# An attention and MLP kernel: the values of three batches loaded as fp32 on a second ring and cast on chip, and a query's two copies on one engine

## The chip, the cores and the metric

The kernel runs on one core of one Trainium2 chip. The metric is the device time of one execution in microseconds (us); lower is better. All kernels of one call ran on the same chip, beside runs of the kernel before. The experiments come from several calls on several chips; the kernel before had medians of 321.6 to 322.25 us in them, so a difference of a few tenths between runs of different calls says nothing.

TensorE does the matmuls, VectorE (DVE), ScalarE (ACT) and GpSimd (POOL) work on tiles, and SyncE (SP) only issues transfers. The program fixes the order of each engine's instructions, and in these traces what stands behind a waiting instruction on VectorE, ScalarE or GpSimd waits too (6.6 us on ScalarE in x14). "Ring" is the queue of transfers that one engine fills; GpSimd's ring is q0 in the profile, SyncE's is q1.

## The reference

Eight batches of causal attention with a window, then an MLP over all 4608 tokens:

```python
# q, k, v: (8 batches, 8 heads, 576 tokens, 64)
# heads 0-3: 0 <= i-j < 32 ("plain"); heads 4-7: 0 <= i-j < 128, (i-j) % 4 == 0 ("dilated")
attn = softmax(where(mask, q @ k.T / 8, -1e9)) @ v
x = attn.transpose(0, 2, 1, 3).reshape(4608, 512)
h = x @ w_in                       # 512 -> 2048
return (h / (1 + exp(-beta * h))) @ w_out
```

## The kernel before

Tokens are handled in nine tiles of 512 for the MLP and in eight batches of 576 for the attention, which runs one batch ahead. `xT` is the attention's output, transposed: 128 partitions, four row blocks of 4608 bf16 columns. As its later columns are free at the start, they also serve as a workshop: the "relay" copies of plain keys and queries lie there. Tile 0 of the MLP is done in two parts of 288 and 224 columns; a "slot" is the work on one of the 16 blocks of 128 hidden columns in such a part, so slot 16 is the first of the second part.

The author writes operations with a wished time `vt`, estimated durations and the engines that could do each. A small simulation (`Plan.run`) then fixes, before the program is built, which engine does what and in which order. Its dependencies decide the order alone. The waits that the chip sees are added afterwards by the framework, from the stretches of tiles that each instruction reads and writes.

```python
rl = xT[0:RT, :, 6 * S:6 * S + R * P].rearrange(          # relay copies
    "p (z x) (T h d) -> p z x T h d", z=2, T=R, h=2)
...
def direct_vd(b, deps, vt):                                # dilated values, cast by the load
    ...
    return [load("POOL", (dst[0:80, 0], rows[0:80]), deps, vt, 320, .35),
            load("POOL", (dst[:, 1], rows[16:CT]), deps, vt, 512, .35)]
...
for hf in range(2):                                        # one copy for each half of a query
    def evac(e, g=g, kind=kind, i=i, hf=hf): ...
    steps[n].append(plan.op([dve(S), act(S)], evac, ...))  # each on VectorE or ScalarE
```

In batches 0 to 2 (`b < DIRECT`) q, k and v come straight from DRAM through GpSimd's ring, which casts fp32 to bf16 on the way, in the order k, q, k, q, values, then w_in and w_out, then batch 1. From batch 3 on, q and k are cast to a scratch in DRAM and read back by transposing loads on SyncE's ring.

The softmax here doesn't subtract the row's maximum and nothing guards it: scores larger than these inputs give would overflow.

## Time and profile before

| | before |
|---|---|
| time, median of 3 runs | 322.11 us (321.36 to 322.4) |
| span of the profiled run | 320.0 us |
| TensorE busy, mean granted clock | 307.9 us (96%), 1.00 |
| useful matmul columns / 2.4 GHz | 286 us |
| GpSimd's ring, SyncE's ring | 20.19 MB, 21.18 MB |

From the page of the kernel before: busy tenths of TensorE, and its granted clock in tenths, in 40 equal slices of 8 us.

```profile
PE   6988999999899999999999999999999999999995
PEclk9999999999999999999999999999999999999999
```

TensorE is busy 80% or more from the second slice to the last but one. The record of its clock begins at 13.2 us and stays at 1.00 until the span's end. The prediction below reads the windows, the timeline and the waits of this kernel.

### The profile page before, as it was taken

To read this page: it belongs to the slowest core of one execution; us is meant where nothing else is said; L and a number is where in the kernel's file an instruction comes from. 1 tells how busy PE (TensorE), PEld (TensorE's weight loads), DVE (VectorE), ACT (ScalarE), POOL (GpSimd) and SP (SyncE) were. 2 spreads that over 40 slices of the span, in tenths; PEclk is the share of its full clock that TensorE was granted. 3 is DMA by queue.
4 is the path that set the end of the run, shared out by engine and by line. 5 is a ranking of instruction groups with operands and counts; after the bars stand their busy time and mean duration, and the time that the engine had idled before them with its cause. 6 is when DMAs were issued, how large, how long until landed. Compare 5 with 4: busy or idle time off the path is not lost.

```text
span 320.0 us, 6224 instructions
## 1 busy us (share of the span) xinstructions
PE 307.9 (96%) x2333; PEld 171.0 (53%) x2333; DVE 210.2 (66%) x488; ACT 181.8 (57%) x346; POOL 123.0 (38%) x158
## 2 busy tenths in 40 slices
PE   6988999999899999999999999999999999999995
PEld 4766777655555545554555454545554444444453
DVE  5578767688988887677778788785875344343300
ACT  2677778677747645574656455645664544545411
POOL 7999753533785445622913652252000000000000
PEclk9999999999999999999999999999999999999999
DMA  6999999999207999799899988993134110100021
GB/s 85 173 208 208 204 172 185 161 178 191 57 2 127 171 213 174 162 172 182 190 171 157 186 193 159 159 221 87 53 88 107 45 55 33 35 33 34 33 100 66
DMA packets 87799, 41.83 MB, mean 131 GB/s; under 512 B 63113, under 2 KB 82457, under 8 KB 87449
## 3 DMA queue, kind: packets, MB, share of 16 engines
q0 software_dynamic: 40544, 20.19, 50.0%
q1 hardware_dynamic: 47080, 21.18, 31.0%
q8 instruction: 18, 0.29, 0.4%
q14 instruction: 13, 0.10, 0.1%
q10 hardware_dynamic: 144, 0.07, 0.1%
HBM read 40.37 MB, written 18.28 MB: 183 GB/s over the span
## 4 chain that ended last, share of the span: by engine, by line
PE 85%; DVE 8%; ACT 3%; issue 2%; POOL 1%; POOLq 0%; DVEq 0%; ACTq 0%
PE bank L730 38%; PE bank L698 35%; PE bank L636 3%; PE bank L565 2%; DVE g L710 2%; PE bank L395 2%; PE bank L576 2%; ACT tnh L705 1%; PE bank L559 1%; DVE xsd L649 1%; POOL st L343 1%; PE bank L666 1%; ACT qd L209 1%; DVE xT L209 1%; ACT pt L603 1%
## 5 line engine op out<-in xcount | busy, mean ns | idle before, releaser
L705 ACT ACTIVATE tnh<-bank,beta_half 128x512 bf16<-128x512 f32 (+2 forms) x160 | 102.5, 645 | 94.2 <-PE bank L698 86.4
L698 PE MATMUL bank<-xT,w_in_bf 128*128 128x512 bf16 (+2 forms) x640 | 145.2, 357 | 1.3 <-ACT xT L209 0.3
L730 PE MATMUL bank<-w_out_bf,g 128*128 128x512 bf16 (+1 forms) x592 | 144.5, 373 | 0.0
L710 DVE SCALAR_TENSOR_TENSOR g<-tnh,bank 128x512 bf16<-128x512 bf16 (+2 forms) x160 | 100.6, 632 | 65.0 <-ACT tnh L705 63.4
L698 PEld LDWEIGHTS <-w_in_bf 128*128 128x128 bf16 x640 | 59.6, 97 | 54.8 <-issue 2.8
L730 PEld LDWEIGHTS <-g 128*128 128x128 bf16 x592 | 54.0, 98 | 50.0
L603 ACT ACTIVATE pt<-bank 128x288 bf16<-128x288 f32 (+1 forms) x112 | 43.9, 447 | 9.7 <-PE bank L565 7.7
L636 PEld LDWEIGHTS <-pt 128*128 128x128 bf16 x448 | 23.5, 97 | 15.8 <-issue 1.4
L747 ACT ACTIVATE osb<-bank 128x512 f32<-128x512 f32 (+2 forms) x34 | 19.8, 583 | 16.6 <-PE bank L730 16.0
L649 DVE TENSOR_TENSOR xsd<-bank,rcp 72x256 bf16<-72x256 f32 x64 | 26.9, 421 | 2.2
L616 POOL TENSOR_TENSOR pt<-pt,mask_d 128x288 bf16<-128x288 bf16 x19 | 13.7, 731 | 38.1 <-ACT pt L603 35.4
L209 POOL COPY kz<-raw 64x1152 bf16<-64x1152 bf16 x8 | 11.9, 1486 | 20.4 <-DMA raw<-s 20.3
L649 DVE TENSOR_TENSOR xsp<-bank,rcp 96x384 bf16<-96x384 f32 x32 | 17.7, 554 | 1.1
L648 DVE RECIPROCAL rcp<-bank 72x4 f32<-72x4 f32 (+1 forms) x96 | 16.8, 175 | 2.2 <-PE bank L636 1.2
L636 PE MATMUL bank<-vd,pt 128*128 128x65 bf16 x256 | 16.4, 193 | 0.3
L565 PE MATMUL bank<-qzd,dk 128*128 128x144 bf16 x128 | 16.4, 232 | 0.0
L209 POOL COPY vd<-st 80x1024 bf16<-80x1024 bf16 (+1 forms) x10 | 10.7, 1084 | 12.5 <-DMA st<-in_v_dram 12.5
L565 PEld LDWEIGHTS <-dk 128*128 128x128 bf16 x128 | 11.0, 101 | 6.9 <-issue 1.7
L343 POOL DMA_DIRECT2D vp<-in_v_dram x9 | 12.5, 1386 | 1.8 <-PE bank L698 1.8
L616 DVE TENSOR_TENSOR pt<-pt,mask_d 128x288 bf16<-128x288 bf16 x29 | 9.1, 341 | 4.2 <-ACT pt L603 4.1
L749 DVE TENSOR_SCALAR osb<-bank 128x512 f32<-128x512 f32 (+1 forms) x4 | 2.4, 592 | 13.8 <-ACT osb L747 13.7
L636 PE MATMUL bank<-vp,pt 128*128 128x65 bf16 x192 | 10.4, 193 | 0.8 <-DVE g L710 0.7
(109 smaller groups left out, 233.3 us busy)
## 6 DMA issues: line engine op xcount, KB each, us to landing
out_dram<-osb SPq DMA_DIRECT2D x35, 256.0 KB, 2.2
s<-in_k_dram POOLq DMA_DIRECT2D x5, 576.0 KB, 6.2
s<-in_q_dram POOLq DMA_DIRECT2D x5, 576.0 KB, 9.2
vp<-in_v_dram POOLq DMA_DIRECT2D x7, 384.0 KB, 13.1
w_out_bf<-in_moe_w_out_dram POOLq DMA_DIRECT2D x2, 1024.0 KB, 21.8
st<-in_k_dram POOLq DMA_DIRECT2D x6, 288.0 KB, 8.5
st<-in_q_dram POOLq DMA_DIRECT2D x6, 288.0 KB, 10.0
x<-xsd SPq DMA_DIRECT2D x10, 144.0 KB
```

The source lines that it names most:

```text
L209: (nc.scalar.copy if e == "ACT" else E[e].tensor_copy)(out=out, in_=in_)
L565: nc.tensor.matmul(sc[:, a, 0:2 * n], lhsT=dk[kv][:, rp, h4, hf * (CT - P):hf * (CT - P) + P], rhs=qzd[kv][:, :, rp, h4, hf * HT:(hf + 1) ...
L603: nc.scalar.activation(out=pt_of(x, j, n).rearrange("p (a b) n -> p a b n", a=2), in_=sc[:, :, 0:2 * n].rearrange("p a (b n) -> p a b n", ...
L616: E[e].tensor_tensor(out=w, in0=w, in1=m, op=ALU.mult)
L636: nc.tensor.matmul(pv[:, a, h2, :], lhsT=pt[x][:, c], rhs=rhs, start=True, stop=True)
L648: nc.vector.reciprocal(out=rc[0:n, 0:m], in_=pv[0:n, :, :, D])
L649: nc.vector.tensor_tensor(out=xs[x, jx][:, a0:a0 + m], in0=pv[0:n, :, :, 0:D], in1=rc[0:n, 0:m].unsqueeze(3).to_broadcast([n, m, 2, D]), o ...
L698: nc.tensor.matmul(bank(g)[:, 0:n], lhsT=w_in_bf[:, kt, fb * P:(fb + 1) * P], rhs=xT[:, kt, xo:xo + n], start=(kt == 0), stop=(kt == NKT - 1))
L705: nc.scalar.activation(out=th[:, 0:n], in_=bank(g)[:, 0:n], func=ACT.Tanh, scale=beta_half[:, fb:fb + 1])
L710: nc.vector.scalar_tensor_tensor(out=g_t[t % 2][:, fb, c0:c0 + n], in0=th[:, 0:n], scalar=1.0, in1=bank(g)[:, 0:n], op0=ALU.add, op1=ALU.mult)
L730: nc.tensor.matmul(bank(g)[:, lo:hi], lhsT=g_t[t % 2][:, fb, tb * P:(tb + 1) * P], rhs=w_out_bf[:, fb, lo:hi], start=(fb == 0), stop=(fb = ...
L747: nc.scalar.mul(out=ob[:, cols], in_=bank(g)[:, cols], mul=0.5)
```

## The change

The intent: GpSimd's ring carries q, k, values and weights one behind another. Take the values of batches 0 to 2 off it, and load them as fp32 through SyncE's ring at the same time, so that the weights come sooner. The fp32 lands in free columns of `xT` and is cast into the bf16 tiles on GpSimd, VectorE or ScalarE. Both halves of a query's copy become one operation on one engine.

```diff
-    rl = xT[0:RT, :, 6 * S:6 * S + R * P].rearrange(
+    rl = xT[0:RT, :, 6 * S + 64:6 * S + 64 + R * P].rearrange(
         "p (z x) (T h d) -> p z x T h d", z=2, T=R, h=2)
+    vp_st = xT[:, :, 3 * S:3 * S + 2 * NI * D].bitcast(FP32).rearrange("p h (i d) -> p h i d", d=D)
+    vd_st = xT[:, :, 3 * S + 2 * NI * D:3 * S + 2 * NI * D + 4 * C * D].bitcast(FP32).rearrange(
+        "p h (f T d) -> p h f T d", f=2, d=D)
 ...
-        return [load("POOL", (dst[0:80, 0], rows[0:80]), deps, vt, 320, .35), ...
+    def load_v(b, deps, vt):            # in this order on SyncE's ring
+        d.append(load("SP", (dst[0:80, 0], rows[0:80]), deps[0], vt, 320, .3, 700))
+        for h4 in range(4): p[h4] = [load("SP", (vp_st[:, h4], src), ..., 192, .21, 1300)]
+        d.append(load("SP", (dst[:, 1], rows[16:CT]), deps[0], vt + .002, 512, .3, 700))
 ...
-                    for hf in range(2):
-                        def evac(e, g=g, kind=kind, i=i, hf=hf):
+                    def evac(e, g=g, kind=kind, i=i):
+                        for hf in range(2):
 ...
+                o = plan.op([("POOL", 780), ("DVE", 930), ("ACT", 820)], spread, ...)   # cast of plain values
 ...
+            if b == 1:   # batch 1's values wait for an MLP result of tile 0
+                gate = [plan.op([("SP", 400)], lambda e: nc.sync.dma_start(
+                    out=gate_t[:], in_=g_t[0][0:1, GATE, 0:16]), gop[0, GATE][:1], base + .04)]
```

(The casting loads of batches 3 to 7 stay.)

## The prediction

> **What bounds the kernel now.** I began with the stretches: busy time of each engine in given windows (columns: window, length, PE, PEld, DVE, ACT, POOL, each with its instructions, then granted TensorE clock, DMA share, GB/s written).
>
> ```profile
> 0.00:20.00 20.00, 15.50 (x163) 12.40 (x164) 11.10 (x31) 10.83 (x22) 17.99 (x38) 1.00 1.15 144
> 20.00:40.00 20.00, 18.12 (x184) 13.32 (x182) 16.14 (x46) 14.64 (x34) 17.39 (x30) 1.00 1.21 207
> 40.00:60.00 20.00, 19.48 (x260) 15.01 (x258) 14.82 (x41) 14.99 (x35) 9.19 (x11) 1.00 1.67 173
> 100.00:200.00 100.00, 99.96 (x718) 51.39 (x716) 78.63 (x182) 56.58 (x106) 45.22 (x46) 1.00 1.11 178
> ```
>
> From 100 us on TensorE has no gap: what comes late there cannot be caught up, what comes early helps. Busy time flatters the start, where fillers (L841) run and matmuls wait for each other, so I also added up columns/2.4 GHz of the useful matmuls (2.4 GHz fits the trace: 512 columns in 0.216 us): 286 us in all, 6.1 of them in the first 20 us, 13.5 in 20 to 40, 17.7, 18.7 and 17.3 in the next three, 19.4 to 19.8 per 20 us after. Of the 320 us span, 34 us are lost: 14, 6.5, 2.3, 1.3, 2.7 in those five, some 3.6 at the end. Only the first 40 us have much to give. There I read the timeline (start, duration, instruction, what ended the wait):
>
> ```profile
> 10.69 1.00 DVE L209 COPY xT<-st 72x1024 bf16<-72x1024 bf16 x2 [0.22 <-DMA st<-in_k_dram]
> 12.76 1.04 ACT L209 COPY xT<-st 72x1024 bf16<-72x1024 bf16 x1 [0.60 <-DMA st<-in_q_dram]
> 23.66 1.14 PE L698 MATMUL bank<-xT,w_in_bf 128*128 128x288 bf16 x8 [0.30 <-ACT xT L209]
> 27.77 8.44 PE L698 MATMUL bank<-xT,w_in_bf 128*128 128x288 bf16 x60
> ```
>
> The first line is the relay copy of plain keys, begun the moment their load lands; queries follow at 12.76. Then come transposes, scores, exponentials, values, and the first MLP matmul at 23.66, which waits for ACT's copy into xT, not for a weight. So the start is bound by the arrival of q and k plus an 11 us chain; weights and values are on time. In the trace the loads land one after another: k, q, k, q at 6.55, 8.50, 10.67, 12.74; v for the dilated heads 13.43 and 14.69, for the plain ones 16.58 and 17.69; w_in 20.85, 23.40, 28.52; w_out 33.45, 38.48; the next keys at 38.84.
>
> **What the Trainium skill says.** "DMA: Bandwidth & Descriptors", section Issuing engines are not separate DMA queues: all initiators use the same 16 engines, a second one saves only issue time. Section Queues, rings and completion order: an engine goes round-robin between its queues packet by packet, some 9 to 17 descriptors each. The trace agrees on the sharing but not on that size. Counting packet records by queue in half microseconds: from 107.5 to 114 us GpSimd's queue and SyncE's queue finish 105 and 108, 98 and 97, 196 and 199, 208 and 206; near 136 us, 9 and 9, 12 and 10, the ones 18 KB, the others 512 B. It is one for one, whatever the size. Small copies on SyncE's ring therefore suffer; in the DMA issues of single windows (KB, us to landing) the same store, alone and beside casts, and a 72 KB pair:
>
> ```profile
> out_dram<-osb SPq DMA_DIRECT2D x1, 256.0 KB, 2.3
> ...
> out_dram<-osb SPq DMA_DIRECT2D x1, 256.0 KB, 7.4
> ...
> x<-xsp SPq DMA_DIRECT2D x2, 72.0 KB, 8.7
> ```
>
> Section SWDGE vs HWDGE vs iDMA: only GpSimd's path casts, hence fp32 and an on-chip cast here. "VectorE: DVE Perf Modes", section The perf-mode tier table: an SBUF copy of bf16 runs at 4x, of fp32 at 2x. The trace has the bf16 one, 1024 columns in 0.42 us; no fp32 copy.
>
> **The change, part by part.** *Removed:* values from GpSimd's ring. For batch 0 that is 17.69 - 12.74 = 5.0 us in front of the weights, for batches 1 and 2 about 9 us behind the keys. But w_in's first piece landed 2.8 us before it was used, so this part buys the first MLP matmul nothing. *Query halves:* the two-engine copy made the halves wait on each other:
>
> ```profile
> DVE qd L209 <- ACT qd L209: 1.4, 1, 1.4
> ACT qd L209 <- DVE qd L209: 1.2, 1, 1.2
> ```
>
> One engine for both (2 x 0.63 on ACT or 2 x 0.75 on DVE) could return 1 to 2 us once, in batch 0. *Added casts:* per batch two of 1024 fp32 columns and two of 768; estimated 0.8 to 1.1 us each on GpSimd (1.03 to 1.1 for 1024 bf16), 0.7 to 1.2 on DVE: about 4 us per batch on engines that have room, 1 us on the first chain.
>
> *Values of batch 0 on SyncE's ring.* A plain-head row is 64 fp32 = 256 B, one packet. Packets per DMA engine: 20 (80 partitions x 4 heads / 16, 1 KB) + 36 + 10 + 3 x 48 = 190 of 256 B + 32 of 1 KB. Against them stand q and k with 288 packets a load, 18 per engine in 2.1 us (115 ns each); w_in 32 in 2.55 us (80 ns) twice, then 32 in 5.1 us (160 ns); w_out 64 in 5.0 us (78 ns) twice. One 256 B packet adds 25 to 35 ns to its partner (76 against 41 ns per 512 B packet, 38 against 14 ns per 128 B packet in those windows). The first 20 go alone before GpSimd's data starts at 3.3 us. Then 72 pairs x 145 ns = 10.4 (to 13.7), 64 x 110 = 7.0 (20.8), 32 x 190 = 6.1 (26.9), 22 x 108 + 32 x 123 = 6.3: the last values land near 33 us instead of 17.7. q and k slip only 1 us, weights end near 38 as now.
>
> *Who waits for that.* The staging areas lie inside xT, as do the relay copies. The built program shows more waits than the author's plan: the dilated values' view runs across all four row blocks of xT, so from first to last element it overlaps nearly everything there. The plain keys' relay copies on ACT and DVE, and the query's on GpSimd, wait for both dilated loads of batch 0; the second is the last on the ring. So the chain that began at 10.7 to 12.8 begins near 33. ACT's list from there, in order: relay 1.04, two exponentials 0.9, kT 0.64, two more 0.9, qd 1.3, two 0.9, four plain ones 1.75, two and two 1.8, copies 0.4: 9.6 us, plus transposes: first MLP matmul near 44, 20 us late. The weights cannot help then.
>
> *Two more enforced waits.* Batch 1's first dilated load waits for the last matmul of slot 5 in the first half of tile 0, and slot 6's second matmul waits for its landing: issue, 2 us latency, 320 KB, so 3.5 to 4.5 us of idle TensorE. The second dilated load (512 KB) waits for slot 15's last matmul and the second matmul of slot 16 for it: 3.5 us. For batch 2 there is work between (some 30 matmuls): about 1 us. Together 8.5 us, in a stage paced by ACT's tanh (0.50 us a slot), so it is not made up.
>
> *Sum.* +20 + 8.5; less about 1 for the query halves, less about 5 of the 6.3 us lost between 40 and 100 us, since keys and weights will then be there early: +22, so 344 us. If the rings share time rather than packets, the values land near 15 (5 to 6 us of data, doubled, and SyncE's issue), the first MLP matmul comes 3 us late: +3 + 8.5 - 1 - 4 = 328.5.
>
> **Rivals.** (a) *The intended gain.* Values land by 15, the weights 3 to 5 us earlier, and enforced waits fall where ACT is the pacer: 312 to 318. For: PE loses 20 us before 40; the ring is now serial. Against: no weight is waited for at 23.66; each enforced wait is between neighbours on TensorE's list. (b) *Time shared, not packets:* 326 to 331. For: the skill's larger packets would give small copies a better share. Against: the counts above. (c) *Hidden anyway:* the delay is absorbed by ACT-bound slots and later gaps, 319 to 326. Against: 20 us of lost gaps after 20 us cannot absorb more than some 6. (d) *Full starvation*, nothing recovered: 350.
>
> **Range and chances.** I give the main account (338 to 349) about 0.7, (b) 0.17, (a) and (c) 0.13; the middle of that is 341. 8 in 10 within 325 to 350. Faster by over 2% (below 315.7) 0.05, within 2% 0.12, slower 0.83.
>
> **What would show it.** Right: plain keys' relay copies ended by a DMA of in_v near 30 us; batch 0's second dilated load issued early with 20 us or more to landing; first MLP matmul above 40; two idle stretches of TensorE of 3 to 4 us ended by in_v in tile 0; from some 100 us on nothing changed. Wrong: values of batch 0 landing before 16, or relay copies that begin at 11 to 13; then the sum falls to (a) or (b). If TensorE shows no gap ended by in_v in tile 0, the enforced waits were mis-read.

## The result

| | before | changed |
|---|---|---|
| median | 322.25 us (321.36 to 322.89, 4 runs) | 362.99 us (361.23 to 364.41, 4 runs) |
| ratio | 1 | 1.1264, 95% interval 1.1207 to 1.1321 |
| span of the profiled run | 320.0 us | 361.1 us |
| TensorE's mean granted clock | 1.00 | 0.934 |

A ratio here is the mean time of one kernel's fast runs over that of the other's of the same rounds, so not quite the ratio of the medians quoted.

The change costs 41 us. Windows of the changed kernel, with the columns of the prediction's first fence:

```profile
0.00:20.00 20.00, 9.76 (x81) 7.49 (x81) 5.99 (x20) 3.93 (x6) 10.10 (x26) 0.78 1.01 180
20.00:40.00 20.00, 8.56 (x97) 7.54 (x98) 6.59 (x11) 8.00 (x18) 8.49 (x13) 0.54 0.99 173
40.00:60.00 20.00, 14.52 (x138) 9.86 (x134) 13.02 (x38) 10.68 (x24) 13.61 (x25) 0.91 0.64 115
60.00:80.00 20.00, 14.20 (x183) 12.16 (x184) 10.81 (x24) 12.33 (x28) 8.50 (x10) 0.83 0.74 139
80.00:100.00 20.00, 15.37 (x173) 11.69 (x173) 13.38 (x37) 12.05 (x24) 7.68 (x9) 0.83 0.73 120
```

TensorE's busy time falls in all five windows, not in the first two alone, and the clock is below 1.00 in each. The relay copies and the first MLP matmul, from the timeline:

```profile
29.49 1.04 ACT L210 COPY xT<-st 72x1024 bf16<-72x1024 bf16 x1 [17.42 <-DMA xT<-in_v_dram]
29.51 0.42 DVE L210 COPY xT<-st 72x1024 bf16<-72x1024 bf16 x1 [16.72 <-DMA xT<-in_v_dram]
```

In the kernel before, the first of these copies began at 10.69, and its wait was ended by the keys that it copies. Here the wait is ended by a load of values, which the copy does not touch. The chain of waits (start, duration, what), cut to the pieces that are not matmuls of the MLP in a row:

```profile
7.73 21.65 DMA xT<-in_v_dram
29.49 1.05 ACT xT L210
...
43.76 0.66 PE bank L726 x4
...
49.19 3.64 DMA xT<-in_v_dram
...
59.63 3.81 DMA xT<-in_v_dram
...
71.24 5.32 DMA xT<-in_v_dram
...
77.68 1.05 POOL xT L210
78.75 4.90 DMA xT<-in_v_dram
...
146.20 4.42 DVE pt L644 x4
```

The first MLP matmul is at 43.76 (before: 23.66). GpSimd, which also issues batch 1's keys, is held up behind the values as well; its first issue of them, before and then changed, with its relay copy ahead of it:

```profile
20.45 0.77 POOL L343 DMA_DIRECT2D st<-in_k_dram  x1
```

```profile
31.32 1.03 POOL L210 COPY xT<-st 72x1024 bf16<-72x1024 bf16 x1 [19.43 <-DVE vd L210]
...
38.28 0.76 POOL L346 DMA_DIRECT2D st<-in_k_dram  x1
```

After the start, the chain falls on values in flight four more times (49 to 84 us), and late, at 146 us, on VectorE's masks.

Of the transfers issued in the first 30 us (KB each, median us to landing), first a part of batch 0's plain values in the kernel before, then plain heads and queries in the changed one:

```profile
vp<-in_v_dram POOLq DMA_DIRECT2D x1, 288.0 KB, 7.3
```

```profile
xT<-in_v_dram SPq DMA_DIRECT2D x3, 192.0 KB, 12.3
st<-in_q_dram POOLq DMA_DIRECT2D x2, 288.0 KB, 9.5
```

The smaller pieces take longer to land, although their ring carries values alone.

I added up the useful matmul columns of both traces as the prediction did, and took how far each is behind the clock on the wall (columns / 2.4 GHz is the least time that they need):

| until | before, us lost | changed, us lost | excess | what lies in between |
|---|---|---|---|---|
| 50 us | 21.2 | 38.8 | 17.6 | late first chain |
| 70 us | 23.5 | 50.7 | 27.1 | two waits in tile 0, low clock |
| 100 us | 26.8 | 63.3 | 36.5 | two waits of batch 2, low clock |
| 160 us | 27.9 | 68.7 | 40.8 | masks at 146 us |
| end | 34.3 | 75.4 | 41.1 | |

The step from 100 to 160 us shows a thing that I had not reckoned with. VectorE's masks (L644) usually take 0.30 to 0.36 us:

```profile
144.55 0.31 DVE L644 TENSOR_TENSOR pt<-pt,mask_d 128x288 bf16<-128x288 bf16 x1 [0.24 <-ACT pt L631]
146.09 3.12 POOL L210 COPY kz<-raw 64x1152 bf16<-64x1152 bf16 x2 [13.52 <-PE bank L604]
146.12 1.77 DVE L644 TENSOR_TENSOR pt<-pt,mask_d 128x288 bf16<-128x288 bf16 x2
147.81 2.81 DVE L644 TENSOR_TENSOR pt<-pt,maske_PP 128x384 bf16<-128x384 bf16 x2
```

While GpSimd copies, two masks take 1.77 and the next two 2.81 us. Over the whole trace, masks with no GpSimd copy beside them took 0.35 us on average (60 of them), those mostly overlapped by one 0.99 us (10 of them). The Trainium skill has this in "SBUF — State Buffer", section SBUF: two separate sides: VectorE and GpSimd share a pair of ports under an exclusive lock that is held for a whole instruction. The trace fits that (0.35 against 0.99 us); no run here takes the copies away, so the lock as the reason is not shown.

### The profile page after: what moved, and what is told of

Read it like the earlier page. It is cut to its first block, busy times and chain, and to the rows that moved or that the text cites. A ratio compares the mean times of both kernels' runs of the same rounds, so it can differ in the third digit from the quotient of the medians.

```text
span 361.1 us, 6269 instructions
## 1 busy us (share of the span) xinstructions
PE 317.9 (88%) x2338; PEld 177.9 (49%) x2338; DVE 218.0 (60%) x494; ACT 185.4 (51%) x348; POOL 113.3 (31%) x146
## 4 chain that ended last, share of the span: by engine, by line
PE 79%; DMA 11%; DVE 4%; SPq 2%; ACT 2%; issue 1%; POOL 0%; ACTq 0%; DVEq 0%; POOLq 0%
PE bank L726 35%; PE bank L758 34%; DMA xT<-in_v_dram 11%; PE bank L664 3%; SPq L346 2%; PE bank L593 2%; PE bank L409 2%; PE bank L604 1%; DVE pt L644 1%; DVE xT L210 1%; DVE xsd L677 1%; PE bank L694 1%; PE bank L598 1%; ACT tnh L733 1%; PE bank L587 1%
## 5 line engine op out<-in xcount | busy, mean ns | idle before, releaser
L726 PE MATMUL bank<-xT,w_in_bf 128*128 128x512 bf16 (+2 forms) x640 | 151.5, 369 | 7.8 <-DMA xT<-in_v_dram 7.3
L726 PEld LDWEIGHTS <-w_in_bf 128*128 128x128 bf16 x640 | 61.3, 102 | 61.0 <-issue 5.5
L664 PEld LDWEIGHTS <-pt 128*128 128x128 bf16 x448 | 24.7, 100 | 24.2 <-issue 9.5
L210 POOL COPY kz<-raw 64x1152 bf16<-64x1152 bf16 x9 | 13.4, 1485 | 32.0 <-DMA raw<-s 18.3
L409 PE MATMUL bank<-ident_b,xT 72*128 72x72 bf16 x96 | 5.4, 216 | 16.5 <-ACT xT L210 15.7
L644 DVE TENSOR_TENSOR pt<-pt,mask_d 128x288 bf16<-128x288 bf16 x39 | 15.3, 418 | 4.0 <-ACT pt L631 3.9
L644 POOL TENSOR_TENSOR pt<-pt,mask_d 128x288 bf16<-128x288 bf16 x9 | 6.6, 736 | 32.9 <-ACT pt L631 31.0
L210 POOL COPY xT<-st 72x1024 bf16<-72x1024 bf16 x5 | 5.1, 1037 | 33.7 <-DVE vd L210 19.4
L210 ACT COPY xT<-st 72x1024 bf16<-72x1024 bf16 x4 | 4.2, 1044 | 21.8 <-DMA xT<-in_v_dram 21.7
L409 PEld LDWEIGHTS <-xT 72*128 72x128 bf16 x96 | 4.7, 110 | 17.4 <-ACT xT L210 15.8
```

The source lines that it names most:

```text
L210: (nc.scalar.copy if e == "ACT" else E[e].tensor_copy)(out=out, in_=in_)
L409: nc.tensor.transpose(tp[:, n], src, ident_b[0:RT, 0:RT])
L644: E[e].tensor_tensor(out=w, in0=w, in1=m, op=ALU.mult)
L664: nc.tensor.matmul(pv[:, a, h2, :], lhsT=pt[x][:, c], rhs=rhs, start=True, stop=True)
L726: nc.tensor.matmul(bank(g)[:, 0:n], lhsT=w_in_bf[:, kt, fb * P:(fb + 1) * P], rhs=xT[:, kt, xo:xo + n], start=(kt == 0), stop=(kt == NKT - 1))
```

## The experiments

**First question: which part of the change costs what?** Theory A: false waits (the program waits for a transfer whose data it does not use), made by where the staging areas lie, together with the late landing of batch 0's values on the second ring, and enforced waits in batches 1 and 2 (each load waits for a matmul, and the next matmul for the load). Rival B: the values are simply late. Rival C: the added casts and issues load the engines.

### x1_places: other places in xT, nothing else

```diff
-    rl = xT[0:RT, :, 6 * S + 64:6 * S + 64 + R * P]...
-    vd_st = xT[:, :, A0:A0 + 4 * C * D].bitcast(FP32)...          # strided over four row blocks
+    rl = xT[0:RT, 2:4, A0:A0 + 2 * R * P]...                      # row blocks 2 and 3
+    vd_st = xT[:, 0:2, A0:A0 + 8 * C * D].bitcast(FP32)...        # one half per row block, 0 and 1
```

> Same transfers, rings and casts as the changed kernel; only the staging areas move inside xT, so that each dilated half, each plain head and each relay area is one contiguous stretch of columns of its own. The built program then has no wait of TensorE and no wait of a relay copy on a values transfer. Theory A (false waits from the strided view): relay copies begin at 11 to 13 us again, no gap of TensorE ended by in_v in tiles 0 and 1; what is left is the true lateness of the values (last landing near 29 us), so the first MLP matmul near 31 to 33 and the time 326 to 334. Rival B (the values' lateness alone makes the loss, the places do not matter): 350 or more, first MLP matmul still above 40. Rival C (the added casts and SyncE's issues load the engines): 350 to 360.

Measured: 340.93 us (ratio 1.0592), 22 us less than the changed kernel. Timeline:

```profile
12.64 1.04 ACT L210 COPY xT<-st 72x1024 bf16<-72x1024 bf16 x1 [0.46 <-DMA st<-in_k_dram]
24.08 0.83 POOL L210 CAST vp<-xT 128x768 bf16<-128x768 f32 x1 [6.95 <-DMA xT<-in_v_dram]
```

The relay copies begin with their keys again, and TensorE's list of waits no longer has a values load. The waits were thus no need of the data: the framework takes a strided view from its first to its last element, and that stretch covered the relay areas and the live columns of three row blocks. The first MLP matmul comes at 34.7: what holds it is a true wait now, for values that land up to 29 us. The time was expected at 326 to 334, so 341 is a miss: 19 us are left, more than the late start.

### x2_d1first: false waits kept, the last load moved to the front

```diff
 d.append(load("SP", (dst[0:80, 0], rows[0:80]), ...))
+if b == 0: d.append(load("SP", (dst[:, 1], rows[16:CT]), ...))   # then the plain heads
```

> Places as in the changed kernel, so all false waits stay; but the second dilated load of batch 0 is issued directly after the first, ahead of the plain values' small packets. Theory A with starvation: that load lands near 10 us, the relay copies begin at 11 to 13, the first MLP matmul comes when the plain values land, 31 to 33 (10 us earlier than 43.8), the gaps at batches 1 and 2 stay: 346 to 354. If the lateness of that load is not what holds the first chain: 360 to 366 as now. If the rest of the loss hangs on that chain too: below 340.

Measured: 353.62 us (1.0988), inside the range. Relay copies began at 14.35 to 18.22 (expected 11 to 13), the first MLP matmul at 34.0 (expected 31 to 33). So the length of the first wait is that one load's place at the end of a slow ring. The enforced waits stayed and grew (6.6 and 3.2 us in tile 0), as they now come while weights still flow.

### x4_b0 and x5_b12: one half of the values each

```diff
+    BY_SP = (0,)        # x4; in x5: (1, 2). The other direct batches load as in the kernel before
```

> Only batch 0's values go through SyncE's ring as fp32; those of batches 1 and 2 through GpSimd's ring with the cast, as in the kernel before. Theory A: first MLP matmul near 43 as in the changed kernel, none of the gaps ended by in_v at 49, 60, 71 and 79 us: 340 to 347 (+20 for the start, minus up to 3 recouped later). If the gaps of batches 1 and 2 are only the start's delay showing elsewhere: 358 to 364.

> The other half: batch 0's values through GpSimd's ring as before, those of batches 1 and 2 through SyncE's as in the changed kernel. Theory A: first MLP matmul near 24 as before, two gaps of 3.5 to 4 us in tile 0 and two of about 5 us before batch 2's relay copies and values: 336 to 346. If the waits of batches 1 and 2 cost little without the late start: 320 to 328. If the two halves add up, the excess over 322 of this run and of the one before it sum to about 41 us.

Measured: x4 347.33 us (1.0783), x5 353.57 us (1.0977). Together 25 + 31.5 = 57 us over the kernel before, not 41: x4's range was missed by 0.3 us, x5's by 7.6, and the halves do not add up. Waits of TensorE in x5 (us in total, times, longest):

```profile
PE bank L746 <- DMA xT<-in_v_dram: 15.1, 2, 8.5
PE bank L429 <- DMA xT<-in_v_dram: 9.5, 1, 9.5
```

In x5 the first two waits fall at 28 and 42 us, beside the weights, and take 6.6 and 8.5 us; in the changed kernel, later by its own late start, they met idle rings and took 3.6 and 3.8. So a late start hides part of the second cost; that the rings' company is the reason is argued from these times. Without the values of batches 1 and 2 on the ring, x4 has no wait for them and loses 7.9 us from 50 to 100 us, where the changed kernel loses 24.5.

**Second question: what are the 19 us left in x1?**

### x3_halves and x7_places_b12

x3 is the kernel before with the one-engine query copy alone. x7 is x1 with batch 0's values on GpSimd's ring again (`BY_SP = (1, 2)`).

> The kernel before with one part of the change alone: both halves of a query's copy on one engine. The prediction's figure: 1 us less at most, 319 to 322. Rival: one engine then carries 1.3 to 1.5 us in a row where two shared it, so the start's chain is longer by up to 1 us: 322 to 325.

> Staging in places of its own, batch 0's values through GpSimd's ring as before, only those of batches 1 and 2 as fp32 through SyncE's. If x1's remaining 19 us are part late start (about 8.5, from the values of batch 0) and part batches 1 and 2 (about 10, the next keys' loads issued late by GpSimd behind casts, and slowed by the values beside them): 329 to 336. If all of the rest is the late start: 320 to 325. If the intended gain exists at all once the false waits are gone, it must show here: below 319.

Measured: x7 327.38 us (1.018), under its first range and far below x1: batch 0's values on the second ring cost 340.9 - 327.4 = 13.5 us. Not all of that is the late start: by the count of useful columns x1 is 11.3 us behind x7 at 100 us, and the rest comes with a stretch of 4.42 us on VectorE's masks at 126 us, which x7 has not. x3 328.87 us (1.0218): both ranges missed, 7 us slower. Its start did gain: first MLP matmul at 22.23 against 23.66. The loss is elsewhere; the longest wait of TensorE and the timeline of x3:

```profile
PE bank L697 <- DMA xT<-x: 5.0, 1, 5.0
```

```profile
176.61 0.68 POOL L343 DMA_DIRECT2D s<-in_k_dram  x1
177.14 9.85 SPq L431 DMA_TRANSPOSE xT<-x  x2
...
190.05 5.00 PE L697 MATMUL bank<-xT,w_in_bf 128*128 128x512 bf16 x16 [5.00 <-DMA xT<-x]
```

At 177 us GpSimd issues batch 7's casting loads just before SyncE issues batch 5's transposing loads into `xT`. Issuing those took 9.85 us and landing 12.9, and TensorE stood still for 5 us. In the kernel before, the plan had put the casting loads at 190 us, behind them. That this collision is the cause is tested in x19.

### x9_places_true: the plan told of the true landings

```diff
-    p[h4] = [load("SP", (vp_st[:, h4], src), deps[1], vt + .001, 192, .21, 1300)]
+    late = (6100, 9000, 10200, 12400)[h4] if b == 0 else 0
+    p[h4] = [load("SP", (vp_st[:, h4], src), deps[1], vt + .001, 192, .21, 1300, 1100 + late)]
```

> As x1 (places of their own), and the author's plan is told when batch 0's values really land (12.8 to 28.4 us instead of the 5.6 to 15.0 it reckoned with), which only changes the order of the instructions on each engine: the casts no longer stand ahead of other work on GpSimd, VectorE and ScalarE. If in-order engines blocked behind those casts are a third cost: TensorE's wait of 7.9 us for the beta transposes (behind GpSimd's cast) goes, and the time falls from 341 to 331 to 338. If the values' landing itself sets the start: 339 to 342.

Measured: 344.91 us (1.0708), 4 us slower than x1 and above both ranges. The 7.9 us wait for the beta transposes went, as expected, but the first MLP matmul came only 1 us earlier (33.65), and TensorE waited 7.8 us for keys instead. My theory that blocked orders were a third cost of several us at the start found no support: with the order changed, the start hardly moved, as the landing had not. The new order made a wait of its own, so the theory is not excluded.

### x10_two and x11_b12_two: the query copy on two engines again

> The whole change, but with the query's halves copied by two engines again as in the kernel before. If x3's 7 us are a cost of the one-engine copy itself and add up: 354 to 358. If they came from one late collision that another order of instructions makes or not (x3's hole at 185 to 190 us, not in the changed kernel, which has its own at 146 to 151): anything from 358 to 367, and the hole at 146 to 151 may move or go.

> As x7 (places of their own, batch 0's values on GpSimd's ring, those of batches 1 and 2 as fp32 on SyncE's), with the two-engine query copy of the kernel before. If the one-engine copy costs 7 us here too: 319 to 322, the best version of the change, level with the kernel before. If x7's excess comes from batches 1 and 2 (first loads beside the weights, GpSimd behind late casts until 50 us): 325 to 330.

In both the diff is the query part of the change, turned back.

Measured: x10, the whole change with the old copy, 365.65 us (1.1361), 2.7 us *slower* than the change; the two ran in different calls, their runs overlap (363.4 to 366.7 and 361.2 to 364.4), and the intervals of their ratios just do not (1.1327 to 1.1395 and 1.1207 to 1.1321). x11, x7 with the old copy, 327.31 us (1.0191), the same as x7. So the copy saves some 2.7 us in the change, costs 7 in the kernel before, and does nothing in x7. One edit with three signs points to the order that it makes, not to the copy: in the kernel before, to the collision (x19). And x7's 5.5 us over the kernel before are not the copy's either.

### x12_one_ring and x13_weights_after: is it the second ring?

```diff
-    d.append(load("SP", (dst[0:80, 0], ...     # x12: every values load of batches 0 to 2; and no gate
+    d.append(load("POOL", (dst[0:80, 0], ...
```

```diff
-    o = load("POOL", (w_in_bf[...]), [], -7.3 + .01 * n, ...)             # x13
+    o = load("POOL", (w_in_bf[...]), ld[0]["vd"] + ld[0]["vp"][3], -7.3 + .01 * n, ...)
```

> Places of their own and the on-chip casts for batches 0 to 2 as in x1, but the fp32 values loaded through GpSimd's ring, behind q and k and ahead of the weights, as in the kernel before. The second ring is then the only thing taken away. If the lateness of batch 0's values comes from the second ring's small packets taking turns with large ones: its values land by 19 to 21 us, the first MLP matmul comes at 24 to 28, and the time is 326 to 334. If the casts and their places in the engines' orders are the cost: 338 or more.

> As x1, but the weights' loads wait for batch 0's last values to land, to measure the values' packets without company: after q and k end at 15 us, the rest of the values should be in by 18 to 21 us instead of 28.4 if they were held up by one-for-one turns with the weights' packets; still 26 or later if the small packets are slow by themselves. The time is not the point: the weights come late, 335 to 350.

Measured: x12 330.35 us (1.0283): the values land by 19.03, the first MLP matmul comes at 24.45. The fp32, the casts and the places are those of x1. The ring differs, and what goes with it: the values stand behind q and k and ahead of the weights, and batch 1's loads have no gate. 10.6 us go. x12 also bounds rival C: with the casts and with a stretch of 4.42 us on the masks it is 8.7 us over the kernel before, not 41. x13 (one run, state unknown, 339.71 us): in this kernel the plan put the weights behind a cast that waits for values, so they were issued at 15.64, behind three loads of batch 1's keys and queries. Its values' packets ended by 16.7 us instead of 29.0. Packet records that ended per microsecond, by ring:

```
                      changed kernel        x13
                      q0     q1             q0     q1
12.0 to 13.0 us      122    535             69    818
17.0 to 18.0 us      136    136            252      0
18.0 to 19.0 us      131    133            210      0
19.0 to 20.0 us      129    130            277      0
```

With weights in company the two rings finish packet for packet. Where q and k thin out (12 to 13 us), the small packets go at 818 a microsecond. They are not slow; they are made to take turns. One thing these rows do not show: from 21 to 29 us the counts of the changed kernel are 19 to 45 on q1 against 94 to 189 on q0. A transfer ends with one 4-byte packet for each of the 16 DMA engines; 12 of the last load's had come by 24.0 us, the last four at 28.4 to 29.1. From 24 to 27 us these four take q1's packets singly, each engine one in every 0.21 us. So the landing that everybody waits for is that of four engines, some 4 to 5 us behind the rest; why they lag is not known.

**Third question: the rest of x7, and the collision.**

### x14_b12_nopool and x15_behind_k

```diff
-    [("POOL", 780), ("DVE", 930), ("ACT", 820)]       # x14: fp32 casts off GpSimd
+    [("DVE", 930), ("ACT", 820)]
-    out=gate_t[:], in_=g_t[0][0:1, GATE, 0:16]        # x15: the gate reads batch 1's keys
+    out=gate_t[:], in_=ks[0:1, 4, 0:16]
```

> As x7 (own places, batch 0's values on GpSimd's ring, batches 1 and 2 as fp32 through SyncE's), but these fp32 casts are given to VectorE and ScalarE only, so that GpSimd does not stand in a cast that waits for late values ahead of the issue of batch 2's keys (51.9 us in x7 against 46.2 in the kernel before). If that order makes x7's excess: keys of batch 2 issued by 47 us, time 320 to 324. If the values' packets beside the keys and weights make it: 326 to 330. If VectorE or ScalarE then stand in those casts instead: 328 or more.

> As x7, but SyncE's loads of batch 1's values wait until batch 1's first keys have landed (the gate reads these keys in place of an MLP result), so no values' packets run beside the weights and few beside the keys. If those packets make x7's 5.5 us: the keys land at 39 to 46 us as in the kernel before, time 320 to 324. If the on-chip casts that wait for values, which now come later, make it: 328 to 334. The plan also learns the later start, so the order changes with it.

Measured: x14 333.11 us (1.0347), x15 333.81 us (1.0359); both worse than x7. In x14 (the dilated values' casts were moved too) ScalarE now stands where GpSimd stood:

```profile
ACT vp L211 <- DMA xT<-in_v_dram: 6.6, 1, 6.6
```

In x15 batch 1's keys landed at 39.3 to 46.3 us, as in the kernel before (38.8 to 45.1), so the packets were off their way. But now the values of both batches run beside batch 2's queries, which land up to 60.7 instead of 59.0, and TensorE waited 3.9 us for a load of them (55.1 to 58.9); a mask collision of 4.4 us came on top. So each cure moved the wait. That late casts block the engine they stand on is shown (x14); how x7's 5.5 us divide between that and the packets beside the keys is not settled. By the count of useful columns x7 is behind the kernel before by 1.9 us at 40 us, 5.2 at 60 and 5.5 at 160, so they arise before 60 us.

### x16_halves_b0, x17_behind and x19_behind

x16 is the kernel before with the one-engine copy in batch 0 only. x17 and x19 are x3 with batch 7's casting loads behind batch 5's transposing loads: x17 in the plan alone, x19 with a wait that the chip sees.

```diff
+    # x17
+    cs = [cast(b, z, ... + ([xcopy[5, 0, 0], xcopy[5, 0, 1]] if b == 7 else []), ...)]
+    # x19: GpSimd reads what the last transposing load writes
+    if b == 7: behind += [plan.op([("POOL", 60)], lambda e: nc.gpsimd.tensor_copy(
+        out=probe[:], in_=xT[0:1, 3, 5 * S + S // 2:5 * S + S // 2 + 16]), [xcopy[5, 0, 0], xcopy[5, 0, 1]], b - 2)]
```

> The kernel before with the one-engine query copy in batch 0 only. x3 was 1.6 us ahead of the kernel before at 50 us and lost it later. If its loss lies in later collisions that the plan's order happens to make: a gain of 1 to 2 us may stay, 320 to 321, or another collision takes it, 322 to 328; the start (first 40 us) must be ahead by about 1.4 us either way.

> As x3, with one order changed: the casting loads of batch 7, which x3 issues at 176.6 us together with batch 5's transposing loads into xT (12.9 us until they landed, TensorE idle for 5.0 us), stand behind these in the plan, as they happen to in the kernel before. If that collision makes x3's loss: the 5 us wait for the transposing loads goes, 321 to 325. If the copy itself costs the time: 327 to 330 as x3.

> As x3, with a small copy on GpSimd that reads what batch 5's last transposing load writes, ahead of batch 7's casting loads, so these are issued only when the transposing loads have landed. If the collision makes x3's loss: transposing loads issued at about 177 us land within 7 us instead of 12.9, TensorE's wait of 5 us for them goes or shrinks below 1.5, time 322 to 326. If batch 7 then comes late by as much: 327 to 331. If they take 12 us without the casting loads beside them: the collision is not the cause.

Measured: x16 325.01 us (1.0116): its first MLP matmul was at 22.26, and the gain was lost again. The profiled run, with 328.66 us the slowest of six (the others took 323.9 to 326.1), has another wait of 4.1 us between 170 and 180 us; whether the faster runs have it too is not known. x17 329.0 us (1.0219): a miss, since the plan's dependency is no wait on the chip; the loads still went out together, and the 5 us wait stayed. x19 320.16 us (0.9932, interval 0.988 to 0.9983). Its timeline:

```profile
179.69 2.86 SPq L432 DMA_TRANSPOSE xT<-x  x2
184.87 0.19 POOL L806 COPY probe<-xT 1x16 bf16<-1x16 bf16 x1 [5.64 <-DMA xT<-x]
185.01 0.58 POOL L344 DMA_DIRECT2D s<-in_k_dram  x1
```

Alone, the two transposing loads were issued in 2.86 us instead of 9.85, and 5.2 us after the first issue they had landed, instead of 12.9; TensorE's wait is gone. The profiled runs differ by 5.2 us (325.1 and 319.9), which is that wait of 5.0; the medians differ by 8.7, as the runs of both fall into two groups some 3 us apart (x19: 318.6 to 318.8 and 321.6 to 322.1). The time is below the expected 322 to 326. x19: the interval lies just below 1, a gain of some 0.7%, and two of its four runs took as long as the kernel before. No version here is clearly faster than that one.

### x6_warm and x6b_warm: TensorE kept busy through the gaps

```diff
+    def keep_warm(g, n):       # n filler matmuls of 256 columns into the bank in use
+    # 110 (x6) or 160 (x6b) ahead of batch 0's first relay transposes, 30 ahead of slot 6, 30 ahead of slot 16
```

> The changed kernel with filler matmuls put where TensorE would stand idle: 110 ahead of the first relay transposes of batch 0, 30 ahead of slot 6 and 30 ahead of slot 16 in tile 0. They end before the wait ends (if they do not, the run is a miss). If the granted clock of 0.5 after each of these idle stretches costs time of its own: the clock of these stretches reads 1.00, the time falls by 3 to 7 us, to 356 to 360. If the stages after the gaps are paced by ScalarE and VectorE anyway, or the clock record means nothing: 361 to 364 as now.

> As x6 (the changed kernel with fillers where TensorE stands idle in the first tile), with 160 instead of 110 ahead of the first relay transposes, so that these find the clock up. If the low clock after the first idle stretch costs time too: the clock reads 1.00 from 24 to 45 us, first relay to first MLP matmul takes 13 us as in the kernel before instead of 14.3, time 357 to 360.5. If ScalarE and VectorE pace that chain: 360 to 362 as x6.

Measured: x6 360.82 us (1.1206), a miss for the first gap, as its fillers ended 4.7 us too early. x6b 359.36 us (1.1153): 3.6 us less than the changed kernel. Windows of the changed kernel, then of x6b (the third figure from the end is the clock):

```profile
30.00:36.00 6.00, 4.56 (x48) 3.70 (x49) 4.08 (x5) 4.48 (x10) 4.54 (x9) 0.50 1.15 191
63.00:69.00 6.00, 5.51 (x52) 4.84 (x53) 2.75 (x5) 3.30 (x6) 1.77 (x2) 0.50 0.50 91
```

```profile
30.00:36.00 6.00, 5.16 (x72) 4.30 (x71) 3.70 (x6) 4.74 (x11) 4.34 (x9) 1.00 1.17 195
63.00:69.00 6.00, 5.06 (x85) 4.55 (x82) 5.24 (x9) 5.53 (x12) 3.03 (x6) 1.00 0.53 67
```

After an idle stretch the clock is 0.50; in the changed kernel 16 transposes took 0.96 us at 64 us and 0.52 us at 98 us. From the first relay copy to the first MLP matmul x6b took 12.9 us (29.69 to 42.57) against 14.3 (29.49 to 43.76), although its fillers overran the copy's end by some 1.2 us. "TensorE: Matmul & The Clock Gate", section What's actually happening, says that the clock starts at half and that activity releases it, idle windows of about 3.4 us taking it away again. The runs agree in the main: fillers of 256 columns took 0.42 us at 2 us and 0.27 us at 45 us, and the record of the changed kernel's clock changes in steps of 3.41 us or multiples. But TensorE need not stand still that long: after a gap of 2.34 us (148.9 to 151.2) the clock was 0.50 for 3.4 us as well. So an idle gap of TensorE costs its length and then some: 3.6 us here for the gaps that x6b filled.

## Why the prediction was wrong, step by step

The direction and the first two costs were right; the time was predicted at 341 (325 to 350) and was 363. The step that failed is what comes after tile 0's two waits: the prediction let batch 2's waits cost about 1 us, won 5 us back, and had nothing change from some 100 us on. Measured: 9.4 us lost, nothing won back, 4.3 us lost late.

- **What bounds the kernel before, and what the change could not buy:** right. The weights were never waited for; x12, with the values as fp32 on the old ring, starts nearly like the kernel before (24.45). The prediction's list of lost time adds up to some 30 of the 34 us; the missing 3.9 lie between 100 and 300 us, which it calls free of gaps, and change nothing in its argument.
- **One for one, so the values land near 33:** right in kind, 29.4 in fact, and without foreseeing that four of the 16 engines would end it. The rival of rings that share time instead is out: it had the values land near 15.
- **False waits, first MLP matmul near 44:** the waits were right, and x1 shows them as the cause: they are worth 22 us of the 41. That 43.76 lies so near 44 is luck: the values came 3.6 us before the 33 predicted, and the chain from there took 14.3 us and not 11, part of it at half clock. The term of +20 measured 17.6.
- **Two enforced waits in tile 0, 3.5 to 4.5 and 3.5 us:** right: 3.64 and 3.81. (The latency of 2 us in that sum is an estimate; 8 KB took 1.7 us to land in the kernel before.) With the low clock behind them they stand for 9.5 us of the table, where the sum had 7.5.
- **"For batch 2 there is work between (some 30 matmuls): about 1 us":** this failed. The chain has 5.3 and 4.9 us there, TensorE's longest gap is 5.5 us (78.8 to 84.3), and the excess grew by 9.4 us from 70 to 100 us. I had looked at TensorE's own list between the two ends of the wait. But each of the two loads waits for work of other engines on the old contents, and then a relay copy on GpSimd and VectorE's copies into `xT` stand behind its landing, falsely too (they wait 2.6 and 5.4 us for it): three engines in a row, each in order.
- **"Less about 5 of the 6.3 us lost between 40 and 100 us, since keys and weights will then be there early":** this failed as well. Nothing was won back. The weights landed at 39.2 (38.5 before), and batch 1's keys at 43.2 to 49.7 instead of 38.8 to 45.1: GpSimd issues them, its relay copy could begin only at 31.3 us, and they went out at 38.3 to 40.4 (20.45 to 22.6 before).
- **Query halves, -1:** the sign was right inside the change (x10: 2.7 us, hardly clear of the spread), and the start gains 1.4 us in x3. That the same edit makes the kernel before 7 us slower was not foreseen.
- **Not in the sum at all:** the half clock after each gap (3.6 us by x6b, part of the three excesses above) and the mask collision at 146 us (4.4 us). The prediction said that from some 100 us on nothing would change. Stretches of 4.42 to 4.44 us on the masks stand in the chains of x1, x4, x9, x10, x12, x15 and x6b as well, and not in those of the kernel before, x2, x3, x5, x7, x11 or x14: whether one comes depends on the order that an edit gives to the late batches. Which part of the change brings it was not tested.

With the sizes of the trace the sum is 17.6 (start) + 9.5 (tile 0) + 9.4 (batch 2) + 4.3 (until 160 us, the masks) + 0.3 = 41. By experiments it is 22 (places) + 13.5 (batch 0's values on the second ring, and the masks with them) + 5.5 (the rest, x7) = 41. The two divisions cut the same loss in different ways; x4 and x5 show that its parts overlap, so neither is a price list.

## What to carry to other kernels

Before a tile's free columns are lent out, list what the strided view covers from its first to its last element: a wait follows for all of it, and a staging area per contiguous stretch removes it with the same transfers (x1: 22 us). A second ring did not bring data sooner here: small packets that took turns with large ones landed at 29 us instead of 16.7, so look at what the other ring carries at that moment. When in-order engines follow a fixed plan, count a delay's consequences through every engine that stands behind it, and check an edit's gain at the place where it should arise (here the first MLP matmul) apart from the total, since the order of everything later changes with it.

## What the Trainium skill lacked or had wrong

- "DMA: Bandwidth & Descriptors", section Queues, rings and completion order, has an engine drain some 9 to 17 descriptors of one row before it switches. Here the records of two busy rings end one for one, 1 KB against 256 B or 1 KB: 136 and 136, 131 and 133, 129 and 130 in three microseconds, and on the four engines that end last they start singly, every 0.21 us. It does not say that a ring of small descriptors is therefore starved: the same values were in at 16.7 us without the weights and at 29 us beside them.
- The same page gives no cost for transposing loads beside casting ones. Two of them took 9.85 us to issue and 12.9 to land beside five casting loads, and 2.86 and at most 5.2 us without (x3, x19).
- "SBUF — State Buffer", section SBUF: two separate sides, has the lock between VectorE and GpSimd, but no figure for such a kernel: masks of 0.35 us on average became 0.99 us beside GpSimd's copies.
- "TensorE: Matmul & The Clock Gate", section What's actually happening, has the clock fall after an idle window of about 3.4 us; a gap of 2.34 us was followed by the half clock in the changed kernel.
- "VectorE: DVE Perf Modes" gives tiers for an fp32 copy; the cast of 1024 columns from fp32 to bf16 took 0.69 us on VectorE and 1.03 us on GpSimd in the changed kernel.
- No page has the false waits of a strided view: 22 us here.
